# Attention feeding a feed-forward layer: scores in four chunks issued two at a time, tails padded to full tiles, one transpose for both tails, all engines in program order

## The chip, the cores and the metric

The kernel runs on one core of one Trainium2 chip. The metric is device time in microseconds (us), the median of several executions. The profile and the trace are those of one execution; their span is about 2 us shorter than the time of the same execution. Engines are named as in the profile: PE is the tensor engine's matmuls, PEld its weight loads, DVE the vector engine, ACT the scalar engine, POOL GpSimd, SP the Sync engine, whose queue (SPq) issues most transfers.

## The reference

Attention with a forget gate over 8 batches of 8 heads, 576 positions, 64 columns a head, followed by a feed-forward layer with SiLU over all 4,608 tokens:

```python
scores = q @ k.T / 8 + (cum[i] - cum[j])        # causal; cum = cumsum(log f)
attn   = softmax(scores)
x      = (attn @ v), heads side by side         # 4608 x 512
h      = x @ w_in                               # 512 x 2048
out    = (h * sigmoid(h)) @ w_out               # 2048 x 512, float32
```

Inputs are float32; the kernel computes in bf16. 576 is 4 tiles of 128 and a tail of 64.

## The kernel before

Work goes by pairs of heads, numbered 0 to 31, four to a batch. For each pair: load and cast q and k, transpose them on PE, copy the transposes to SBUF (`qkT`), multiply them (`scores`), take exp on ACT into `u`, mask on DVE. For each two pairs, `den` sums the weights, DVE takes reciprocals (`rec`), and eight transfers spread them over partitions (`rb<-rec`). `num` multiplies by v, and DVE multiplies by `rb` into `xT`. Between these steps the loop calls `fill`, which issues pieces of the feed-forward layer: 144 pieces of the first matmul (`hp`, then tanh on ACT and `gt` on DVE, the "gate work") and 144 of the second (`po`). A piece is four matmuls of 512 columns. `fill` can give nothing before the first batch is finished, which is at the end of pair 4.

Each partition gets four neighbouring rows of q or k (1 KB runs), so the transposes come out permuted, and the DVE copy puts the columns in order with a strided write:

```python
    def transposes(n):
        tp = psc.tile([P, 2, 1024], BF16, name="tp", tag="sc")
        for i in range(2):                       # q, k
            for j in range(NJ):
                nc.tensor.transpose(tp[:, i, j * P : (j + 1) * P], src[:, i, j, :], ident_bf[:, :])
            nc.tensor.transpose(                 # the tail, 64 rows
                tp[:, i, SM:S], tail[:, i, p * P : (p + 1) * P], ident_bf[:ST, :ST])
        t = qktp.tile([P, 2, S], BF16, name="qkT", tag="qkT")
        for i in range(2):
            nc.vector.tensor_copy(
                out=t[:, i, 0:SM].rearrange("r (p j) -> r j p", j=NJ),
                in_=tp[:, i, 0:SM].rearrange("r (j p) -> r j p", j=NJ))
        nc.vector.tensor_copy(out=t[:, :, SM:S], in_=tp[:, :, SM:S])
    # [cut] scores: three chunks of 512 columns, then the 64x64 tail "sd" with its own exp
    # [cut] den, num: tail matmuls with 64 rows
    for n in range(NU):                          # shortened
        scores(n, 0); fill(1)
        # [cut] casts of pair n+1 (POOL), loads of pair n+4 and of the next batch (SP)
        scores(n, 1); fill(1)
        scores(n, 2); fill(2)
        transposes(n + 1); fill(1)
        if n % 2 == 1:
            fill(1); den(n // 2); rec_part(n // 2, 0); fill(1); rec_part(n // 2, 1); fill(1)
        elif n >= 2:
            num(n - 2); fill(1); num(n - 1); fill(2); finished(n - 1)
```

Only PE runs in the order of the program; the Tile framework orders the other four queues.

The softmax here doesn't subtract the row's maximum and nothing guards it: scores larger than these inputs give would overflow.

## Time and profile before

448.99 us (3 runs, 445.46 to 449.27). The page of the profile, parts 1 and 2 (busy time with share of the span; then tenths busy in 40 equal slices of 11.2 us):

```profile
PE 390.3 (87%) x3013; PEld 177.7 (40%) x3013; DVE 290.5 (65%) x406; ACT 204.7 (46%) x312; POOL 97.5 (22%) x149
...
PE   2236676899979999999989998999899989999996
...
PEclk9999999999999999999999999999999999999999
DMA  8995959975666365425642423250203020400011
```

PE is 80% to full from slice 8 on, but for two slices, and 20 to 70% busy before; DMA is busiest just where PE is not.

From the trace I take the start of each pair, which is the start of its first scores matmul. Pairs 7 to 30 are regular: two pairs without gate work and two with it alternate. In the windows view, one such group of four pairs (columns: stretch, length, then busy time of each engine, PE clock, DMA share, GB/s):

```profile
175.58:188.77 13.19, 11.62 (x92) 5.40 (x92) 12.25 (x18) 7.62 (x12) 2.28 (x4) 1.00 0.33 85
188.77:199.05 10.28, 10.28 (x91) 4.50 (x91) 6.90 (x10) 4.27 (x6) 1.17 (x2) 1.00 0.37 106
199.05:210.78 11.73, 11.42 (x91) 5.23 (x92) 6.80 (x10) 4.27 (x6) 3.00 (x4) 1.00 0.48 140
210.78:221.07 10.29, 10.29 (x92) 4.50 (x92) 7.15 (x13) 7.23 (x12) 4.55 (x7) 1.00 0.83 193
```

Three of the four are filled by PE. The first, with gate work and two `num`, has DVE busy for 12.25 of 13.19 us.

The timeline of PE around a transposition (start, duration, line, operation, count). The durations shown overlap (190.38 + 1.04 lies beyond 191.35), so the distance from one start to the next is what counts:

```profile
190.38 1.04 PE L423 MATMUL po<-w_out_bf,gt 128*128 128x512 bf16 x4
191.35 0.39 PE L278 MATMUL sc<-qkT 64*128 64x320 bf16 x4
...
191.82 1.90 PE L423 MATMUL po<-w_out_bf,gt 128*128 128x512 bf16 x8
193.56 0.39 PE L235 MATMUL tp<-ident_bf,qkb 128*128 128x128 bf16 x4
193.88 0.20 PE L238 MATMUL tp<-ident_bf,qkt 64*128 64x64 bf16 x1
194.01 0.40 PE L235 MATMUL tp<-ident_bf,qkb 128*128 128x128 bf16 x4
194.34 0.20 PE L238 MATMUL tp<-ident_bf,qkt 64*128 64x64 bf16 x1
194.47 0.82 PE L423 MATMUL po<-w_out_bf,gt 128*128 128x512 bf16 x3
```

Eight full `po` matmuls before full transposes take 1.74 us, so four take 0.87; the four before 64-row scores take 0.97 (190.38 to 191.35). The change from `128*128` to `64*128` costs about 0.1 us. Below, this is called a mode switch, and also a drain; both names stand for this distance between starts, and what PE does in it the trace does not show. The transposes of the pair take 0.91 us (193.56 to 194.47).

The groups of DVE and ACT that matter (count, busy us, mean ns of one, idle before):

```profile
L285 ACT ACTIVATE u<-sc 128x1024 bf16<-128x1024 f32 x96 | 97.9, 1026 | 50.9 <-PE sc L278 39.8
L243 DVE COPY qkT<-tp 128x512 bf16<-128x512 bf16 x64 | 79.2, 1322 | 27.4 <-PE tp L238 27.4
L343 DVE RECIPROCAL rec<-dn 128x288 f32<-128x288 f32 x32 | 61.2, 1936 | 4.5 <-PE dn L331 4.5
```

And the first reciprocals, in the timelines of DVE and of the SP queue:

```profile
35.52 3.77 DVE L343 RECIPROCAL rec<-dn 128x288 f32<-128x288 f32 x2 [0.16 <-PE dn L331]
...
44.24 0.72 DVE L378 TENSOR_TENSOR xT<-nm,rb 128x576 bf16<-128x576 f32 x1
```

```profile
27.93 0.47 SPq L75 DMA_DIRECT2D kf<-in_k_dram  x1
39.31 5.02 SPq L351 DMA_DIRECT2D rb<-rec  x8
```

The reciprocals end at 39.3 us; the SP queue has issued nothing since 28.4 and issues `rb` at once.

### The profile page before, as it was taken

Reading aid. Unit: us, or ns where it says so; the run is one execution under the profiler, and the core shown is the slowest. Engines: PE = TensorE matmul, PEld = TensorE weight load, DVE = VectorE, ACT = ScalarE, POOL = GpSimd, SP = SyncE. Lnnn points to the kernel's source line nnn. Section 1 sums busy time; section 2 is a strip of 40 time slices with the busy share of each in tenths; the row PEclk is TensorE's granted clock in tenths of the full one; section 3 lists DMA queues with packets and bytes.
Section 4 is the critical chain, followed back from the end, with each engine's and each line's share of the span. In section 5 each row is a group of like instructions: output and inputs, shape, how many; then the busy total and the mean of one; then the engine's idle time right before and its main releaser. Section 6 shows DMA issues by size and latency. Waiting matters only on the chain.

```text
span 448.4 us, 7690 instructions
## 1 busy us (share of the span) xinstructions
PE 390.3 (87%) x3013; PEld 177.7 (40%) x3013; DVE 290.5 (65%) x406; ACT 204.7 (46%) x312; POOL 97.5 (22%) x149
## 2 busy tenths in 40 slices
PE   2236676899979999999989998999899989999996
PEld 1113332344434444444444444444444444444442
DVE  4668553966598649964996489647965794374310
ACT  3222323654464437443754375437543754264421
POOL 6573250361242151214221422111111000000000
PEclk9999999999999999999999999999999999999999
DMA  8995959975666365425642423250203020400011
GB/s 234 211 212 129 217 91 204 269 168 155 176 145 152 102 172 128 124 95 162 139 123 89 130 72 101 72 148 26 53 25 101 26 53 25 123 1 24 25 70 70
DMA packets 79156, 52.03 MB, mean 116 GB/s; under 512 B 49872, under 2 KB 70352, under 8 KB 79120
## 3 DMA queue, kind: packets, MB, share of 16 engines
q1 hardware_dynamic: 74896, 47.35, 40.4%
q0 software_dynamic: 4224, 4.19, 5.8%
q8 instruction: 23, 0.38, 0.4%
q14 instruction: 13, 0.11, 0.1%
HBM read 36.85 MB, written 9.44 MB: 103 GB/s over the span
## 4 chain that ended last, share of the span: by engine, by line
PE 54%; DVE 25%; ACT 11%; issue 5%; DMA 3%; SPq 1%; POOL 0%; DVEq 0%; ACTq 0%; POOLq 0%
PE po L423 28%; PE hp L396 11%; ACT u L285 7%; DVE qkT L243 7%; DVE gt L405 6%; DVE rec L343 6%; PE nm L366 5%; PE sc L278 3%; DVE u L298 3%; PE tp L235 3%; PE dn L331 2%; DMA rb<-rec 2%; ACT osb L432 2%; ACT th L404 2%; DVE u L302 1%
## 5 line engine op out<-in xcount | busy, mean ns | idle before, releaser
L396 PE MATMUL hp<-xT,w_in_bf 128*128 128x512 bf16 x576 | 141.7, 385 | 12.2 <-DVE gt L405 6.8
L423 PE MATMUL po<-w_out_bf,gt 128*128 128x512 bf16 x576 | 137.9, 380 | 0.0
L405 DVE SCALAR_TENSOR_TENSOR gt<-th,hp 128x512 bf16<-128x512 bf16 x144 | 94.9, 675 | 53.4 <-ACT th L404 53.0
L404 ACT ACTIVATE th<-hp 128x512 bf16<-128x512 f32 x144 | 86.1, 602 | 89.1 <-PE hp L396 81.6
L285 ACT ACTIVATE u<-sc 128x1024 bf16<-128x1024 f32 x96 | 97.9, 1026 | 50.9 <-PE sc L278 39.8
L243 DVE COPY qkT<-tp 128x512 bf16<-128x512 bf16 x64 | 79.2, 1322 | 27.4 <-PE tp L238 27.4
L396 PEld LDWEIGHTS <-w_in_bf 128*128 128x128 bf16 x576 | 50.9, 98 | 67.4 <-issue 16.5
L423 PEld LDWEIGHTS <-gt 128*128 128x128 bf16 x576 | 50.6, 98 | 58.9 <-issue 5.7
L432 ACT ACTIVATE osb<-po 128x512 f32<-128x512 f32 x36 | 21.5, 597 | 97.3 <-PE po L423 92.0
L343 DVE RECIPROCAL rec<-dn 128x288 f32<-128x288 f32 x32 | 61.2, 1936 | 4.5 <-PE dn L331 4.5
L95 POOL CAST qkb<-qf 128x512 bf16<-128x512 f32 x31 | 19.1, 615 | 197.3 <-issue 114.9
L278 PE MATMUL sc<-qkT 64*128 64x512 bf16 (+4 forms) x320 | 41.0, 323 | 23.6 <-ACT u L285 11.9
L298 DVE TENSOR_TENSOR u<-u,mask 128x768 bf16<-128x768 bf16 x32 | 22.2, 692 | 32.1 <-ACT u L285 32.1
L278 PEld LDWEIGHTS <-qkT 64*128 64x128 bf16 x320 | 13.5, 97 | 66.3 <-issue 51.2
L378 DVE TENSOR_TENSOR xT<-nm,rb 128x576 bf16<-128x576 f32 x32 | 23.8, 744 | 17.9 <-PE nm L366 11.5
L366 PE MATMUL nm<-u,vp 128*64 128x64 bf16 (+4 forms) x512 | 30.0, 264 | 4.4 <-DVE qkT L247 3.5
L366 PEld LDWEIGHTS <-vp 128*64 128x64 bf16 x512 | 19.5, 117 | 22.6 <-DVE qkT L247 10.6
L235 PE MATMUL tp<-ident_bf,qkb 128*128 128x128 bf16 x256 | 27.6, 236 | 0.7 <-ACT u L285 0.5
L235 PEld LDWEIGHTS <-qkb 128*128 128x128 bf16 x256 | 18.2, 104 | 8.6 <-issue 0.5
L95 POOL CAST qkb<-kf 128x512 bf16<-128x512 f32 x32 | 20.6, 643 | 3.0 <-DMA kf<-in_k_dram 3.0
L331 PE MATMUL dn<-u,w_bf 128*32 128x64 bf16 (+4 forms) x512 | 16.0, 261 | 5.9 <-DVE u L298 5.9
L331 PEld LDWEIGHTS <-w_bf 128*32 128x32 bf16 (+1 forms) x576 | 11.3, 99 | 17.1 <-issue 13.1
(79 smaller groups left out, 150.8 us busy)
## 6 DMA issues: line engine op xcount, KB each, us to landing
rb<-rec SPq DMA_DIRECT2D x128, 72.0 KB, 2.0
out_dram<-osb SPq DMA_DIRECT2D x36, 256.0 KB, 2.0
qf<-in_q_dram SPq DMA_DIRECT2D x32, 256.0 KB, 3.1
kf<-in_k_dram SPq DMA_DIRECT2D x32, 256.0 KB, 3.3
w_in_bf<-in_moe_w_in_dram POOLq DMA_DIRECT2D x4, 512.0 KB, 8.3
w_out_bf<-in_moe_w_out_dram POOLq DMA_DIRECT2D x4, 512.0 KB, 11.2
qtf<-in_q_dram SPq DMA_DIRECT2D x8, 128.0 KB, 3.9
ktf<-in_k_dram SPq DMA_DIRECT2D x8, 128.0 KB, 4.0
```

The source lines that it names most:

```text
L95: ins = engs[i].tensor_copy(out=t2[:, i, :, :].rearrange("p j (h d) -> p h j d", d=D), in_=t[:, :, :].rearrange("p h (j d) -> p h j d", d=D),)
L235: nc.tensor.transpose(tp[:, i, j * P : (j + 1) * P], src[:, i, j, :], ident_bf[:, :])
L243: nc.vector.tensor_copy(out=t[:, i, 0:SM].rearrange("r (p j) -> r j p", j=NJ), in_=tp[:, i, 0:SM].rearrange("r (j p) -> r j p", j=NJ),)
L278: nc.tensor.matmul(sc[:, i, col : col + q1 - q0], lhsT=t[r, 1, kb * P : (kb + 1) * P], rhs=t[r, 0, q0:q1], start=True, stop=True,)
L285: nc.scalar.activation(out=u[:, :, c * 512 : (c + 1) * 512], in_=sc[:, :, :], func=ACT.Exp, scale=scale)
L331: nc.tensor.matmul(dn[32 * j : 32 * j + 32, q0:q1], lhsT=w_bf[r, kb, bh : bh + 1].to_broadcast([nk, 32]), rhs=rhs, start=(kb == 0), stop=( ...
L343: nc.vector.reciprocal(out=rec[:, r], in_=dn[:, r])
L366: nc.tensor.matmul(nm[i * D : (i + 1) * D, q0:q1], lhsT=v_t[r, p, :] if kb == NM else vp[:, kb, 2 * p + i, :], rhs=(ut[r, :] if kb == NM e ...
L396: nc.tensor.matmul(hp[:, :], lhsT=w_in_bf[:, cc, fc * P : (fc + 1) * P], rhs=xT[:, cc, t0 : t0 + TG], start=(cc == 0), stop=(cc == NCC - 1),)
L404: nc.scalar.activation(out=th[:, :], in_=hp[:, :], func=ACT.Tanh, scale=0.5)
L405: nc.vector.scalar_tensor_tensor(out=gt[:, fc, :], in0=th[:, :], scalar=1.0, in1=hp[:, :], op0=ALU.add, op1=ALU.mult,)
L423: nc.tensor.matmul(po[:, :], lhsT=gt[:, fc, tb * P : (tb + 1) * P], rhs=w_out_bf[:, fc, :], start=(fc == 0), stop=(fc == NFC - 1),)
```

## The change

It aims at fewer 64-row visits on PE and a cheap qkT copy. q and k are loaded in natural order (256-byte runs), so one contiguous copy of 1,152 columns suffices. The q tail and k tail share a full 128-row transpose. The 64-row tail of `den` and `num` becomes a full tile whose upper half is masked to zero. Scores are 1,600 columns in four chunks of 400, issued two and two, with no separate tail. ACT copies the denominators out of PSUM before DVE takes reciprocals. All five engines run in program order.

```diff
-    ctx.enter_context(tc.manual_schedule(engines={mybir.EngineType.PE}))
+    ctx.enter_context(tc.manual_schedule(engines=set(ORDERED)))     # PE, ACT, DVE, POOL, SP
 # load_qk
-            t = stage.tile([P, 2, NJ * D], FP32, ...)
-            nc.sync.dma_start(out=t[:, :, :],
-                in_=src[b, 2 * p : 2 * p + 2, 0:SM, :].rearrange("h (p j) d -> p h (j d)", j=NJ))
+            t = stage.tile([P, NM, 2, D], FP32, ...)
+            for i in range(2):
+                nc.sync.dma_start(out=t[:, :, i, :],
+                    in_=src[b, 2 * p + i, 0:SM, :].rearrange("(c p) d -> p c d", p=P))
 # transposes
-            nc.tensor.transpose(tp[:, i, SM:S], tail[:, i, ...], ident_bf[:ST, :ST])
-        [three copies, two of them strided]
+        nc.tensor.transpose(tp[:, SM : SM + P], tbf[b][:, p * P : (p + 1) * P], ident_bf[:, :])
+        nc.vector.tensor_copy(out=t[:, :], in_=tp[:, 0:QKW])
 # den
+        nc.scalar.activation(out=rec[:, :], in_=dn[:, 0:S], func=ACT.Copy)
 # loop
         scores(n, 0)
+        scores(n, 1)
         fill(1)
 [cut: casts and loads of later pairs; w_in still at pair 2, w_out at pair 5 instead of 6]
-        scores(n, 1)
         fill(1)
         scores(n, 2)
-        fill(2)
+        scores(n, 3)
+        fill(2 if n % 2 == 0 else 1)
 [cut: also den and num tails, masks, v tails; num(n-2) and num(n-1) now side by side]
```

More of the change, by code (lines that the diff above doesn't have):

```diff
@@ L13 @@
 P = 128
+ET = mybir.EngineType
+ORDERED = (ET.PE, ET.Activation, ET.DVE, ET.Pool, ET.SP)
 @with_exitstack
@@ L59 @@
     pbig = ctx.enter_context(tc.tile_pool(name="pbig", bufs=4, space=bass.MemoryType.PSUM))
-    NJ = SM // P
     qst: dict[int, tuple] = {}
-    tst: dict[int, tuple] = {}
+    tst: dict[int, bass.AP] = {}
     vst: dict[int, list] = {}
@@ L67 @@
     tbf: dict[int, bass.AP] = {}
-    vbf: dict[int, tuple] = {}
+    vbf: dict[int, bass.AP] = {}
     def load_qk(n):
@@ L73, in load_qk @@
         for name, src in (("qf", q), ("kf", k)):
-            t = stage.tile([P, 2, NJ * D], FP32, name=name, tag=name, bufs=4)
-            nc.sync.dma_start(
-                out=t[:, :, :],
-                in_=src[b, 2 * p : 2 * p + 2, 0:SM, :].rearrange("h (p j) d -> p h (j d)", j=NJ),
-            )
+            t = stage.tile([P, NM, 2, D], FP32, name=name, tag=name, bufs=4)
+            for i in range(2):
+                nc.sync.dma_start(
+                    out=t[:, :, i, :],
+                    in_=src[b, 2 * p + i, 0:SM, :].rearrange("(c p) d -> p c d", p=P),
+                )
             ts.append(t)
@@ L82, in load_tails @@
     def load_tails(b):
-        ts = []
-        for name, src in (("qtf", q), ("ktf", k)):
-            t = stage.tile([ST, H, D], FP32, name=name, tag=name)
+        t = stage.tile([P, H, D], FP32, name="qktf", tag="qktf")
+        for i, src in enumerate((q, k)):
             nc.sync.dma_start(
-                out=t[:, :, :], in_=src[b, :, SM:S, :].rearrange("h s d -> s h d")
-            )
-            ts.append(t)
-        tst[b] = tuple(ts)
+                out=t[i * ST : (i + 1) * ST, :, :],
+                in_=src[b, :, SM:S, :].rearrange("h s d -> s h d"),
+            )
@@ L92, in cast_qk @@
+        tst[b] = t
     def cast_qk(n, engs):
-        t2 = conv.tile([P, 2, NJ, 2 * D], BF16, name="qkb", tag="qkb")
+        t2 = conv.tile([P, 2, NM, 2 * D], BF16, name="qkb", tag="qkb")
         for i, t in enumerate(qst.pop(n)):
-            ins = engs[i].tensor_copy(
-                out=t2[:, i, :, :].rearrange("p j (h d) -> p h j d", d=D),
-                in_=t[:, :, :].rearrange("p h (j d) -> p h j d", d=D),
+            engs[i].tensor_copy(
+                out=t2[:, i, :, :], in_=t[:, :, :, :].rearrange("p c h d -> p c (h d)")
@@ L98, in cast_qk, with load_v @@
             )
         qbf[n] = t2
-        return ins
     def cast_tails(b):
-        t2 = conv.tile([ST, 2, H * D], BF16, name="qkt", tag="qkt")
-        for i, t in enumerate(tst.pop(b)):
-            nc.gpsimd.tensor_copy(
-                out=t2[:, i, :], in_=t[:, :, :].rearrange("s h d -> s (h d)")
-            )
+        t2 = conv.tile([P, H * D], BF16, name="qkt", tag="qkt")
+        nc.gpsimd.tensor_copy(out=t2[:, :], in_=tst.pop(b)[:, :, :].rearrange("s h d -> s (h d)"))
         tbf[b] = t2
-    def load_v(b, c, h0, h1):
+    def load_v(b, c):
@@ L111, in load_v @@
         if b not in vst:
             vst[b] = [
-                stage.tile([P, H if i < NM else NP, D], FP32, name=f"vf{i}", tag=f"vf{i}")
-                for i in range(NM + 1)
-            ]
-        if c < NM:
-            nc.sync.dma_start(
-                out=vst[b][c][:, h0:h1, :],
-                in_=v[b, h0:h1, c * P : (c + 1) * P, :].rearrange("h p d -> p h d"),
-            )
-            return
-        for i in range(2):
-            nc.sync.dma_start(
-                out=vst[b][c][i * ST : (i + 1) * ST, h0 // 2 : h1 // 2, :],
-                in_=v[b, h0 + i : h1 : 2, SM:S, :].rearrange("h p d -> p h d"),
-            )
+                stage.tile([P, H, D], FP32, name=f"vf{i}", tag=f"vf{i}") for i in range(NM + 1)
+            ]
@@ L128 @@
+        r = slice(0, P) if c < NM else slice(ST, P)
+        nc.sync.dma_start(
+            out=vst[b][c][r, :, :],
+            in_=v[b, :, c * P : min(S, (c + 1) * P), :].rearrange("h p d -> p h d"),
+        )
     f_sb = setup.tile([BH, S], FP32, name="f_sb")
@@ L134 @@
     for c in range(NM + 1):
-        load_v(0, c, 0, H)
+        load_v(0, c)
     ident_bf = const.tile([P, P], BF16, name="ident_bf")
@@ L144 @@
     mask_t = const.tile([P, ST], BF16, name="mask_t")
-    for i in range(2):
-        make_upper_triangular(nc, mask_t[i * ST : (i + 1) * ST, :], val=1.0, diag=True)
+    nc.gpsimd.memset(mask_t[0:ST, :], 0.0)
+    make_upper_triangular(nc, mask_t[ST:P, :], val=1.0, diag=True)
     xT = const.tile([P, NCC, NT], BF16, name="xT")
@@ L199, with convert_v, k_off @@
     us: dict[int, tuple] = {}
-    def convert_v(b, c, h0, h1, eng):
+    def convert_v(b, c):
         if b not in vbf:
-            vbf[b] = (
-                vpool.tile([P, NM, H, D], BF16, name="vp", tag="vp"),
-                vpool.tile([P, NP, D], BF16, name="v_t", tag="v_t"),
-            )
-        vp, v_t = vbf[b]
-        vf = vst[b][c]
-        if c < NM:
-            eng.tensor_tensor(
-                out=vp[:, c, h0:h1, :],
-                in0=vf[:, h0:h1, :],
-                in1=w_bf[:, c, b * H + h0 : b * H + h1, None].to_broadcast([P, h1 - h0, D]),
-                op=ALU.mult,
-            )
-            return
-        for i in range(2):
-            r = slice(i * ST, (i + 1) * ST)
-            eng.tensor_tensor(
-                out=v_t[r, h0 // 2 : h1 // 2, :],
-                in0=vf[r, h0 // 2 : h1 // 2, :],
-                in1=w_bf[r, NM, b * H + h0 + i : b * H + h1 : 2, None].to_broadcast(
-                    [ST, (h1 - h0) // 2, D]
-                ),
-                op=ALU.mult,
-            )
+            vbf[b] = vpool.tile([P, NM + 1, H, D], BF16, name="vp", tag="vp")
+        vp = vbf[b]
+        r = slice(0, P)
+        if c == NM:
+            r = slice(ST, P)
+            nc.gpsimd.memset(vp[0:ST, NM, :, :], 0.0)
+        n = r.stop - r.start
+        nc.gpsimd.tensor_tensor(
+            out=vp[r, c, :, :],
+            in0=vst[b][c][r, :, :],
+            in1=w_bf[r, c, b * H : (b + 1) * H, None].to_broadcast([n, H, D]),
+            op=ALU.mult,
+        )
+    QKW = 2 * S
+    def k_off(kb):
+        return SM if kb == NM else S + ST + kb * P
     def transposes(n):
@@ L230, in transposes @@
         src = qbf.pop(n)
-        tail = tbf[b]
-        tp = psc.tile([P, 2, 1024], BF16, name="tp", tag="sc")
+        tp = psc.tile([P, 2048], BF16, name="tp", tag="sc")
         for i in range(2):
-            for j in range(NJ):
-                nc.tensor.transpose(
-                    tp[:, i, j * P : (j + 1) * P], src[:, i, j, :], ident_bf[:, :]
-                )
-            nc.tensor.transpose(
-                tp[:, i, SM:S], tail[:, i, p * P : (p + 1) * P], ident_bf[:ST, :ST]
-            )
@@ L241, in transposes @@
-        t = qktp.tile([P, 2, S], BF16, name="qkT", tag="qkT")
-        for i in range(2):
-            nc.vector.tensor_copy(
-                out=t[:, i, 0:SM].rearrange("r (p j) -> r j p", j=NJ),
-                in_=tp[:, i, 0:SM].rearrange("r (j p) -> r j p", j=NJ),
-            )
-        nc.vector.tensor_copy(out=t[:, :, SM:S], in_=tp[:, :, SM:S])
-        qkT[n] = t
-    UW = 3 * 512
-    def u_off(kb, qq):
-        if kb == 0:
-            return qq if qq < SM else 960 + qq - SM
-        if kb == 1:
-            return 512 + qq - 128
-        if kb == 2:
-            return 1024 + qq - 256
-        return 1344 + qq - 384
@@ L261 @@
-    CHUNKS = (
-        ((0, 0, 512, 0),),
-        ((1, 128, 576, 0), (0, 512, 576, 448)),
-        ((2, 256, 576, 0), (3, 384, 576, 320)),
-    )
+            for c in range(NM):
+                o = i * (S + ST) + c * P
+                nc.tensor.transpose(tp[:, o : o + P], src[:, i, c, :], ident_bf[:, :])
+        nc.tensor.transpose(
+            tp[:, SM : SM + P], tbf[b][:, p * P : (p + 1) * P], ident_bf[:, :]
+        )
+        t = qktp.tile([P, QKW], BF16, name="qkT", tag="qkT")
+        nc.vector.tensor_copy(out=t[:, :], in_=tp[:, 0:QKW])
@@ L267, in scores @@
+        qkT[n] = t
+    UO = [0]
+    for kb in range(NM + 1):
+        UO.append(UO[-1] + S - kb * P)
+    UW = UO[-1]
+    CW = UW // 4
     def scores(n, c):
         if c == 0:
-            u = upool.tile([P, 2, UW], BF16, name="u", tag="u")
-            ut = upool.tile([P, ST], BF16, name="ut", tag="ut")
-            us[n] = (u, ut)
-        u, ut = us[n]
+            us[n] = upool.tile([P, 2, UW], BF16, name="u", tag="u")
+        u = us[n]
         t = qkT[n]
         sc = psc.tile([P, 2, 512], FP32, name="sc", tag="sc")
-        for kb, q0, q1, col in CHUNKS[c]:
+        for kb in range(NM + 1):
+            lo, hi = max(UO[kb], c * CW), min(UO[kb + 1], (c + 1) * CW)
+            if lo >= hi:
+                continue
+            q0 = kb * P + lo - UO[kb]
@@ L278, in scores @@
                 nc.tensor.matmul(
-                    sc[:, i, col : col + q1 - q0],
-                    lhsT=t[r, 1, kb * P : (kb + 1) * P],
-                    rhs=t[r, 0, q0:q1],
+                    sc[:, i, lo - c * CW : hi - c * CW],
+                    lhsT=t[r, k_off(kb) : k_off(kb) + P],
+                    rhs=t[r, q0 : q0 + hi - lo],
                     start=True,
@@ L285, in scores @@
         nc.scalar.activation(
-            out=u[:, :, c * 512 : (c + 1) * 512], in_=sc[:, :, :], func=ACT.Exp, scale=scale
+            out=u[:, :, c * CW : (c + 1) * CW], in_=sc[:, :, 0:CW], func=ACT.Exp, scale=scale
         )
-        if c < 2:
+        if c % 2 == 0:
             return
-        sd = pbig.tile([P, ST], FP32, name="sd", tag="big")
-        for i in range(2):
-            r = slice(i * D, (i + 1) * D)
-            nc.tensor.matmul(
-                sd[r, :], lhsT=t[r, 1, SM:S], rhs=t[r, 0, SM:S], start=True, stop=True
-            )
-        nc.scalar.activation(out=ut[:, :], in_=sd[:, :], func=ACT.Exp, scale=scale)
-        d0 = u[:, :, :].rearrange("p i (c x) -> p (i c) x", x=512)[:, :, 0:P]
-        nc.vector.tensor_tensor(
-            out=d0, in0=d0, in1=mask[:, None, :].to_broadcast([P, 6, P]), op=ALU.mult
-        )
-        d1 = u[:, :, 1344 : 1344 + P]
-        nc.vector.tensor_tensor(
-            out=d1, in0=d1, in1=mask[:, None, :].to_broadcast([P, 2, P]), op=ALU.mult
-        )
-        nc.vector.tensor_tensor(out=ut[:, :], in0=ut[:, :], in1=mask_t[:, :], op=ALU.mult)
+        d = [u[:, :, UO[c - 1] : UO[c - 1] + P], u[:, :, UO[c] : UO[c] + P]]
+        for x in d:
+            nc.vector.tensor_tensor(
+                out=x, in0=x, in1=mask[:, None, :].to_broadcast([P, 2, P]), op=ALU.mult
+            )
+        if c == 3:
+            x = u[:, :, UO[NM] : UW]
+            nc.vector.tensor_tensor(
+                out=x, in0=x, in1=mask_t[:, None, :].to_broadcast([P, 2, ST]), op=ALU.mult
+            )
     def q_parts(kb):
@@ L310, in q_parts, with u_part @@
         yield SM, S
+    def u_part(n, i, kb, q0, q1):
+        o = UO[kb] - kb * P
+        return us[n][:, i, o + q0 : o + q1]
     recs: dict[int, bass.AP] = {}
@@ L322, in den @@
                     bh = b * H + 2 * p + i
-                    u, ut = us[n]
-                    r = slice(i * ST, (i + 1) * ST) if kb == NM else slice(0, P)
-                    nk = ST if kb == NM else P
-                    rhs = (
-                        ut[r, :]
-                        if kb == NM
-                        else u[:, i, u_off(kb, q0) : u_off(kb, q0) + q1 - q0]
-                    )
                     nc.tensor.matmul(
                         dn[32 * j : 32 * j + 32, q0:q1],
-                        lhsT=w_bf[r, kb, bh : bh + 1].to_broadcast([nk, 32]),
-                        rhs=rhs,
+                        lhsT=w_bf[:, kb, bh : bh + 1].to_broadcast([P, 32]),
+                        rhs=u_part(n, i, kb, q0, q1),
                         start=(kb == 0),
@@ L337, in den @@
                     )
-        dens[qd] = (dn, recp.tile([P, S], FP32, name="rec", tag="rec"))
+        rec = recp.tile([P, S], FP32, name="rec", tag="rec")
+        nc.scalar.activation(out=rec[:, :], in_=dn[:, 0:S], func=ACT.Copy)
+        dens[qd] = rec
     def rec_part(qd, part):
-        dn, rec = dens[qd]
+        rec = dens[qd]
         r = slice(part * S // 2, (part + 1) * S // 2)
-        nc.vector.reciprocal(out=rec[:, r], in_=dn[:, r])
+        nc.vector.reciprocal(out=rec[:, r], in_=rec[:, r])
         if part == 0:
@@ L358, in num @@
         b, p = divmod(n, NP)
-        u, ut = us.pop(n)
-        vp, v_t = vbf[b]
+        vp = vbf[b]
         nm = psc.tile([P, 1024], FP32, name="nm", tag="sc")
@@ L364, in num @@
                 for i in range(2):
-                    r = slice(i * ST, (i + 1) * ST)
                     nc.tensor.matmul(
                         nm[i * D : (i + 1) * D, q0:q1],
-                        lhsT=v_t[r, p, :] if kb == NM else vp[:, kb, 2 * p + i, :],
-                        rhs=(
-                            ut[r, :]
-                            if kb == NM
-                            else u[:, i, u_off(kb, q0) : u_off(kb, q0) + q1 - q0]
-                        ),
+                        lhsT=vp[:, kb, 2 * p + i, :],
+                        rhs=u_part(n, i, kb, q0, q1),
                         start=(kb == 0),
@@ L376, in num @@
                     )
+        us.pop(n)
         rb = recs.pop(n)
@@ L463 @@
         scores(n, 0)
+        scores(n, 1)
         fill(1)
         if n + 1 < NU:
-            last_cast = cast_qk(n + 1, (nc.gpsimd, nc.gpsimd))
+            cast_qk(n + 1, (nc.gpsimd, nc.gpsimd))
         if n + 4 < NU:
@@ L469 @@
         if n == 2:
-            with tc.issue_after(last_cast.ins):
-                for c in range(NM + 1):
-                    convert_v(0, c, 0, H, nc.gpsimd)
-                for i in range(WQ):
-                    load_w_in(i)
-        if n == 6:
-            with tc.issue_after(last_cast.ins):
-                for i in range(WQ):
-                    load_w_out(i)
+            for c in range(NM + 1):
+                convert_v(0, c)
+            for i in range(WQ):
+                load_w_in(i)
+        if n == 5:
+            for i in range(WQ):
+                load_w_out(i)
         if b + 1 < B:
@@ L482 @@
                 for c in range(NM + 1):
-                    load_v(b + 1, c, 0, H)
+                    load_v(b + 1, c)
             if p == 2:
@@ L486 @@
                 for c in range(2):
-                    convert_v(b + 1, c, 0, H, nc.gpsimd)
+                    convert_v(b + 1, c)
             if p == 3:
                 for c in range(2, NM + 1):
-                    convert_v(b + 1, c, 0, H, nc.gpsimd)
-        scores(n, 1)
+                    convert_v(b + 1, c)
         fill(1)
         scores(n, 2)
-        fill(2)
+        scores(n, 3)
+        fill(2 if n % 2 == 0 else 1)
         if n + 1 < NU:
             transposes(n + 1)
-        fill(1)
+        fill(2)
         if n % 2 == 1:
-            fill(1)
             den(n // 2)
             rec_part(n // 2, 0)
-            fill(1)
+            fill(2)
             rec_part(n // 2, 1)
@@ L506 @@
             num(n - 2)
-            fill(1)
             num(n - 1)
```

## The prediction

> **What bounds it now.** The page gives TensorE (PE) 390.3 us of 448.4 (87%), DVE 290.5, ACT 204.7. The stage table shows PE busy about 48 us of every 50 from 150 on but 5.6 to 14.1 in the first four stretches of 20. Three parts:
> - a start of about 65 us: no feed-forward work yet, each head pair a latency chain (scores, exp, transposes, qkT copies);
> - 27 head pairs bound by PE. In the timeline four pairs repeat every 45.5 us (10.66, 11.35, 10.66, 12.81; the last has gate work and reciprocals, so DVE, at about 11 us, limits it);
> - a feed-forward tail of about 78 us, untouched.
>
> **PE: the change removes mode switches.** [...] four 512-column matmuls take 862 ns before another of their kind, but 969 ns before 64-row scores, so about 107 ns a switch. Per pair, from start times:
> - Transposes: 912 ns now. Full ones start 56 ns apart, but the 64-row tails add about 100 ns going in and out, twice. Nine full ones: about 505. Saves 0.41 us.
> - Scores: seven switches now, four after. Columns stay 1,600. Saves 0.3 us.
> - num tail with 128 rows: one switch less, 0.11; the two num side by side: 0.21 per two pairs; den tail: 0.1 per two pairs.
> Together about 1.0 us a pair, on the critical path while PE binds.
>
> **DVE.** qkT costs 2 x 1.22 + 0.25 us now (512 elements written with stride). One contiguous copy of 1,152 bf16 from PSUM: 0.75 us [...], 1.3 [...] (estimates from the 252 ns for 128 elements and 744 for 576). Masks rise from three operations to five, about +0.25. Net about -1.3 us a pair, which should remove most of each fourth pair's stall of 1.5 to 2 us.
>
> **ACT.** Three exps of 1,024 (1.03 us) plus one of 64 (0.23) become four of 800: 0.84 each by the slope between 602 ns for 512 and 1,026 for 1,024. Even. The denominator's copy adds about 0.65 us per two pairs. ACT reaches about 8.7 us of a 10 us pair with tanh work: tight.
>
> **DMA.** q and k change from 1 KB packets (median 46 ns) to 256 B (18 ns, so 72 per KB): some 49,000 packets and 15 to 25 us of 16-engine time more over the span, most harmful in the first 60 us, where DMA is mostly 80 to 100% busy.
>
> **Sum.** Start: the chain of four exps, transposes and one short copy is about 7.5 us a pair against about 10.5; with DMA and GpSimd contention pair 5 starts near 55 instead of 65. Pairs 5 and 6: 27 instead of 31. 24 pairs at 10.45 instead of 11.43: 251 instead of 274. Tail 77. Total **410 us**, range 397 to 425. Faster by over 2% 0.94, within 0.045, slower 0.015.
>
> **Right or wrong shows in:** a pair's transposes taking about 0.5 us; steady pair periods of 9.6 to 10.8 us; DVE qkT near 0.75 or 1.3 us; first feed-forward matmul at 50 to 58 us; more DMA packets, near 128,000.
>
> **What would make it wrong:** strict program order making ACT or DVE wait at the head of its queue (masks behind the fourth exp, reciprocals before gates); transposes waiting for the third exp after only one filler in odd pairs; 256 B packets or the ordered SP queue delaying the start.

55, 27, 251 and 77 add to 410 us. The 107 ns of a switch rest on the two distances beside them. The 0.75 and 1.3 us for the copy are estimates from two durations of the before trace, 252 ns for a copy of 128 bf16 elements and 744 ns for a multiplication of 576 float32 columns: a fixed 190 ns and 0.96 ns an element fit both if the bf16 copy takes half of that per element, and 1,152 elements then come to 0.74 us, or to 1.30 at the whole. That the copy would go at the half was the assumption; no run had shown it.

## The result, and the profile after

420.95 us (4 runs, 420.44 to 422.15) against 447.23 for the kernel before (4 runs); ratio 0.9416, 95% interval 0.9356 to 0.9476: faster. A ratio here is the mean time of one kernel's fast runs over that of the other's fast runs of the same rounds, so it is not quite the ratio of the medians quoted.

The page after, the same lines:

```profile
PE 359.0 (86%) x3109; PEld 176.8 (42%) x3109; DVE 249.9 (60%) x406; ACT 213.2 (51%) x328; POOL 95.9 (23%) x140
...
PE   1650456989998999899989998999899989999996
...
PEclk9995565999999999999999999999999999999999
DMA  8999699761696179617861696169614021300111
```

The first slices of PE are as empty as before, and now PE's granted clock drops to 0.5 to 0.6 in slices 4 to 7. It does not decide the time: of four runs three show a mean clock near 0.95 and one 1.00, with times of 420.4 to 422.2 and 421.4 us. Why the clock drops here and not in the kernel before, no run tests.

One group of four pairs in the windows view:

```profile
162.02:173.16 11.14, 10.39 (x94) 5.26 (x94) 11.09 (x20) 7.26 (x12) 3.92 (x6) 1.00 0.58 138
173.16:183.91 10.75, 9.61 (x96) 4.54 (x95) 5.52 (x10) 4.98 (x7) 1.31 (x2) 1.00 0.39 95
183.91:194.06 10.15, 10.15 (x96) 5.12 (x95) 5.31 (x10) 4.22 (x6) 1.18 (x2) 1.00 0.40 104
194.06:203.85 9.79, 9.59 (x96) 4.53 (x95) 7.17 (x13) 8.03 (x13) 4.72 (x6) 1.00 1.08 234
```

41.8 us against 45.5. The first fell by 2.05 us, the third by 1.58; the second rose by 0.47, with PE idle for over a microsecond in it. PE around that pair:

```profile
173.16 0.34 PE L247 MATMUL sc<-qkT 64*128 64x400 bf16 x2
174.64 0.35 PE L247 MATMUL sc<-qkT 64*128 64x176 bf16 x4 [1.14 <-ACT u L254]
174.92 1.90 PE L379 MATMUL po<-w_out_bf,gt 128*128 128x512 bf16 x8
...
178.08 0.61 PE L219 MATMUL tp<-ident_bf,qkb 128*128 128x128 bf16 x8
178.53 0.22 PE L220 MATMUL tp<-ident_bf,qkt 128*128 128x128 bf16 x1
178.59 1.89 PE L379 MATMUL po<-w_out_bf,gt 128*128 128x512 bf16 x8
```

The transposes take 0.51 us (178.08 to 178.59) instead of 0.91. The bracket in the second line says that PE was idle for 1.14 us until an exp ended. The groups:

```profile
L254 ACT ACTIVATE u<-sc 128x800 bf16<-128x800 f32 x128 | 101.2, 847 | 53.9 <-PE sc L247 43.9
...
L224 DVE COPY qkT<-tp 128x1152 bf16<-128x1152 bf16 x32 | 24.0, 750 | 4.2 <-PE tp L220 4.1
```

The copies fell from 87 us in all to 24: one copy of 1,152 contiguous elements took 750 ns, where one of 512 strided ones had taken 1,322. Of the prediction's two estimates it is the lower, 0.75 us. ACT's exps took 847 ns (predicted 840).

The start, in the timelines of DVE and the SP queue:

```profile
22.18 3.77 DVE L304 RECIPROCAL rec<-rec 128x288 f32<-128x288 f32 x2 [0.57 <-ACT rec L298]
...
44.72 0.76 DVE L334 TENSOR_TENSOR xT<-nm,rb 128x576 bf16<-128x576 f32 x1 [14.87 <-DMA rb<-rec]
```

```profile
26.20 5.90 SPq L112 DMA_DIRECT2D vf_226<-in_v_dram  x1
32.16 4.12 SPq L77 DMA_DIRECT2D qf<-in_q_dram  x2
...
40.33 5.02 SPq L312 DMA_DIRECT2D rb<-rec  x8
```

The reciprocals end at 26.0 us, 13 us earlier than before. But the queue is stuck: loads for batch 1 that nobody needs yet take up to 5.9 us each to issue, loads of q and k follow, and `rb` goes out at 40.3. The first `xT` is written at 44.7 us; before it was 44.2. Pairs 0 and 1 went from 12.3 and 10.8 us to 4.9 and 5.7, and pair 2 from 10.6 to 23.9. All that the faster pairs won was given back as one wait.

Where the time went (starts of pairs and the span from the trace, us; each rounded by itself):

| | before | after | predicted |
|---|---|---|---|
| start of pair 5 | 64.9 | 65.3 | 55 |
| pairs 5 and 6 | 30.8 | 24.1 | 27 |
| pairs 7 to 30 | 274.9 | 251.2 | 251 |
| pair 31 to the end | 77.6 | 78.2 | 77 |
| span / sum | 448.4 | 418.7 | 410 |

### The profile page after: what moved, and what is told of

The parts are those of the page before. It is cut to its first block, busy times and chain, and to the rows that moved or that the text cites. A ratio compares the mean times of both kernels' runs of the same rounds, so it can differ in the third digit from the quotient of the medians.

```text
span 418.7 us, 8037 instructions
## 1 busy us (share of the span) xinstructions
PE 359.0 (86%) x3109; PEld 176.8 (42%) x3109; DVE 249.9 (60%) x406; ACT 213.2 (51%) x328; POOL 95.9 (23%) x140
## 3 DMA queue, kind: packets, MB, share of 16 engines
q1 hardware_dynamic: 124944, 47.36, 50.1%
## 4 chain that ended last, share of the span: by engine, by line
PE 50%; DVE 17%; SPq 11%; ACT 9%; DMA 6%; issue 5%; POOL 1%; ACTq 0%; DVEq 0%; POOLq 0%
PE po L379 26%; PE hp L352 14%; DVE gt L361 7%; DVE rec L304 6%; ACT u L254 6%; SPq L77 4%; SPq L312 4%; PE nm L325 3%; PE sc L247 3%; PE dn L290 2%; PE tp L219 2%; ACT th L360 2%; DMA out_dram<-osb 2%; SPq L112 1%; DVE u L261 1%
## 5 line engine op out<-in xcount | busy, mean ns | idle before, releaser
L352 PE MATMUL hp<-xT,w_in_bf 128*128 128x512 bf16 x576 | 137.6, 383 | 0.1
L254 ACT ACTIVATE u<-sc 128x800 bf16<-128x800 f32 x128 | 101.2, 847 | 53.9 <-PE sc L247 43.9
L261 DVE TENSOR_TENSOR u<-u,mask 128x256 bf16<-128x256 bf16 x128 | 42.4, 346 | 57.7 <-ACT u L254 57.4
L247 PE MATMUL sc<-qkT 64*128 64x176 bf16 (+5 forms) x512 | 40.0, 269 | 36.2 <-DVE xT L334 20.0
L304 DVE RECIPROCAL rec<-rec 128x288 f32<-128x288 f32 x32 | 61.1, 1934 | 15.7 <-ACT rec L298 15.7
L247 PEld LDWEIGHTS <-qkT 64*128 64x128 bf16 x512 | 20.3, 99 | 67.4 <-issue 63.0
L325 PEld LDWEIGHTS <-vp 128*64 128x64 bf16 x576 | 21.0, 114 | 20.4 <-issue 15.9
L224 DVE COPY qkT<-tp 128x1152 bf16<-128x1152 bf16 x32 | 24.0, 750 | 4.2 <-PE tp L220 4.1
L219 PE MATMUL tp<-ident_bf,qkb 128*128 128x128 bf16 x256 | 21.9, 235 | 3.8 <-ACT u L254 2.9
L103 POOL CAST qkt<-qktf 128x512 bf16<-128x512 f32 x8 | 4.9, 616 | 58.4 <-DMA qktf<-in_k_dram 58.4
L298 ACT ACTIVATE rec<-dn 128x576 f32<-128x576 f32 x16 | 10.4, 651 | 13.1 <-PE dn L290 12.9
```

The costliest lines, as they stand in the source:

```text
L219: nc.tensor.transpose(tp[:, o : o + P], src[:, i, c, :], ident_bf[:, :])
L224: nc.vector.tensor_copy(out=t[:, :], in_=tp[:, 0:QKW])
L247: nc.tensor.matmul(sc[:, i, lo - c * CW : hi - c * CW], lhsT=t[r, k_off(kb) : k_off(kb) + P], rhs=t[r, q0 : q0 + hi - lo], start=True, sto ...
L254: nc.scalar.activation(out=u[:, :, c * CW : (c + 1) * CW], in_=sc[:, :, 0:CW], func=ACT.Exp, scale=scale)
L261: nc.vector.tensor_tensor(out=x, in0=x, in1=mask[:, None, :].to_broadcast([P, 2, P]), op=ALU.mult)
L304: nc.vector.reciprocal(out=rec[:, r], in_=rec[:, r])
```

## The experiments

Twelve kernels ran, all on the same inputs and all accepted by the comparison with the reference. A "group" below is four times the mean of pairs 7 to 30. All times are medians of fast runs; one run of strided_copy, the profiled one, was slow and is left out. The before kernel ran at medians of 449.2 to 449.6 us beside them, so ratios to it compare better than times do.

| kernel | us | ratio to before | pair 3 starts | pair 5 starts | group |
|---|---|---|---|---|---|
| before | 447.23 | 1 | 46.0 | 64.9 | 45.8 |
| after | 420.95 | 0.942 | 45.5 | 65.3 | 41.9 |
| rb_first | 453.19 | 1.005 | 34.8 | 63.4 | 47.7 |
| pack1k_wrong | 418.66 | 0.929 | 42.5 | 62.8 | 41.9 |
| w_in_late | 415.78 | 0.925 | 35.0 | 59.8 | 41.8 |
| before_ordered | 449.69 | 0.999 | 38.8 | 57.4 | 47.3 |
| two_visits | 427.57 | 0.952 | 45.9 | 66.2 | 42.8 |
| one_score | 418.86 | 0.933 | 46.3 | 66.1 | 41.6 |
| strided_copy | 437.67 | 0.976 | (slow profile) | | |
| spread | 406.07 | 0.903 | 34.7 | 55.8 | 41.2 |
| before_short_copy | 433.95 | 0.968 | 41.2 | 58.1 | 44.3 |
| spread_rot | 399.79 | 0.891 | 34.2 | 56.5 | 40.2 |
| spread_odd1 | 399.93 | 0.892 | 34.9 | 55.7 | 40.4 |
| pe_order_only | 432.99 | 0.963 | 58.5 | 75.1 | 42.7 |

### The start: order, packets, or the weight load?

**rb_first** moves loads behind the reciprocals in program order:

```diff
-        if n + 4 < NU: load_qk(n + 4)            # after the casts, early in the pair
-            if p == 0: load_tails(b + 1); [five] load_v(b + 1, c)
+        # at the end of the pair
+        if n + 4 < NU: load_qk(n + 4)
+        if b + 1 < B and p == 1: load_tails(b + 1); [five] load_v(b + 1, c)
```

> After kernel, only the order of the Sync queue changed: the loads of the next batch's tails and v move from the start of each first pair to the end of each second pair, and each pair's q and k loads to the end of the pair, so the broadcast of the first reciprocals (rb) is issued before them. Theory A (the 14.7 us stall of pair 2 is rb standing behind prefetches in the queue): rb is issued within 1 us of the reciprocals, near 26 us instead of 40.3; pair 3 starts at 30 to 36 us instead of 45.5, pair 5 at 52 to 60 instead of 65.3, and the total falls by 5 to 13 us to 408 to 416. Rival B (the DMA engines simply cannot deliver the bytes of the start sooner, whatever the order): pair 5 still starts at 63 to 67 us because a later load is waited for instead, and the total stays within 4 us of 421.

453.19 us, a miss in total, yet theory A held for the stall itself: `rb` was issued at 26.01 us and pair 3 began at 34.8 instead of 45.5. Pair 5 began at 63.4, which is in rival B's range, so this run alone does not exclude B. What went wrong is the edit's own doing. POOL's queue is in order too, and its cast of the next tails comes at a fixed place:

```profile
42.35 0.61 POOL L103 CAST qkt<-qktf 128x512 bf16<-128x512 f32 x1 [16.47 <-DMA qktf<-in_k_dram]
```

POOL now waited 16.5 us for tails that were requested later, with the casts of q and k for the next pair behind it. The same happened once in every batch (one pair in four took 17 us), so the gain was lost several times over. Moving a load means moving what waits for it.

**pack1k_wrong** loads q and k in 1 KB runs as before and leaves the columns permuted. The result is wrong. It passed the comparison all the same; with inputs scaled by 0.1 the scores are tiny, which would explain it, but that was not tested.

```diff
-            t = stage.tile([P, NM, 2, D], ...);  in_=...rearrange("(c p) d -> p c d", p=P)
+            t = stage.tile([P, 2, NM * D], ...); in_=...rearrange("(p j) d -> p (j d)", j=NM)
```

> Wrong result on purpose: the after kernel with q and k loaded four rows to a partition (1 KB packets as in the kernel before) and not put back in order. Everything else has the same shape. Theory C (256 B packets [...] make the start slow): the Sync issues at 26 to 40 us, which took 2.5 to 6 us each, drop below 1.5 us; rb is issued near 30 us; pair 5 starts 6 us or more earlier and the total is 410 to 415. Theory A or B (order, or bytes with the w_in burst): packets matter little, pair 5 moves by less than 4 us, total 417 to 421. Packets in total should fall from 129 thousand to about 80 thousand.

Pair 3 came 3.0 us earlier and pair 5 2.6; 418.66 us, ratio 0.929. So theory C is a small part: `rb` began to issue at 29.7, but its eight issues took 12.1 us, where they took 5.0 in the kernels before and after. The ratio improved by 1.2 points.

**w_in_late** issues the four loads of w_in at pair 4:

```diff
-        if n == 2: ...; [four] load_w_in(i)
+        if n == 4: [four] load_w_in(i)
```

> After kernel with the four w_in loads issued at pair 4 instead of pair 2. Theory D (the 4 MB w_in burst at 22 to 26 us on the GpSimd queue is what fills the DMA engines and so delays rb): pair 2's stall falls from 14.7 us to under 5 and pair 3 starts before 38 us; but the first feed-forward matmul then may wait for w_in, so the total may gain little or lose. If pair 2 still stalls over 10 us, the burst is not the cause.

Pair 3 at 35.0, so theory D holds: without the 4 MB burst the same loads in the same order left the queue free at 29.6 us, when `rb` was issued. The burst then struck pair 4 (18.0 us). Net 415.78 us, ratio 0.925.

Order and burst are thus two handles on one cause: in the first 40 us the DMA engines are loaded to the full (DMA share 1.08 and 1.26 in the first two stretches of 20 us of the after kernel; the view adds the times of packets, so it can exceed 1), and `rb` was late when anything not yet needed was ahead of it: it was issued at 40.3 us in the after kernel, at 29.7 in pack1k_wrong and 29.6 in w_in_late, but at 26.0 in rb_first, where those loads came behind it.

**spread** uses both handles and moves the waiters along:

```diff
             if p == 0: load_tails(b + 1)         # v no longer here
             if p == 2: cast_tails(b + 1)
-                       [two] convert_v(b + 1, c)
-            if p == 3: [three] convert_v(b + 1, c)
+            if p == 3: [five] convert_v(b + 1, c)
 # after rec_part(n // 2, 1)
+            if p == 1 and b + 1 < B: [five] load_v(b + 1, c)
-        if n == 2: [four] load_w_in;  if n == 5: [four] load_w_out
+        w_in parts: one at pair 2, one at 3, two at 4;  w_out parts: two at pair 5, two at 6
```

> After kernel with the start's transfers put in the order of need: v of the next batch is loaded after the first rb of the batch, its casts and multiplications on GpSimd moved one or two pairs later so that its queue does not wait for them, w_in issued in four parts over pairs 2 to 4, w_out over pairs 5 and 6. Theory A plus D (the start is bound by what stands ahead of rb on the DMA engines: unneeded prefetches and the w_in burst): pair 3 starts at 28 to 33 us, pair 5 at 48 to 56, steady groups stay at 41.8, total 405 to 413. Rival B (bytes): pair 5 still starts after 60 us, because w_in or q and k are waited for, total above 416.

406.07 us, ratio 0.903. `rb` goes out when the reciprocals end, and v behind it:

```profile
26.06 5.26 SPq L312 DMA_DIRECT2D rb<-rec  x8
31.42 7.46 SPq L112 DMA_DIRECT2D vf<-in_v_dram  x5
```

Pair 3 began at 34.7, later than the expected 28 to 33, pair 5 at 55.8, at the upper end of what was expected, and rival B is out. Groups fell by 0.7 us as well, which was not expected: the pair with gate work and two `num` went from 11.14 to 10.31 us in most groups. The after trace shows why, in the timelines of DVE, POOL and PE in such a pair, and of DVE in pair 30:

```profile
167.14 0.90 DVE L261 TENSOR_TENSOR u<-u,mask 128x256 bf16<-128x256 bf16 x2
167.97 0.63 DVE L266 TENSOR_TENSOR u<-u,mask_t 128x128 bf16<-128x128 bf16 x1
...
167.28 0.62 POOL L96 CAST qkb<-qf 128x512 bf16<-128x512 f32 x1 [2.50 <-PE tp L220]
167.84 0.67 POOL L96 CAST qkb<-kf 128x512 bf16<-128x512 f32 x1
...
170.51 0.89 PE L325 MATMUL nm<-u,vp 128*64 128x512 bf16 x18 [0.75 <-DVE qkT L224]
...
335.38 0.49 DVE L261 TENSOR_TENSOR u<-u,mask 128x256 bf16<-128x256 bf16 x2
```

POOL's casts of q and k run just while DVE masks. The five masks of the pair then add to 2.17 us instead of 1.35, DVE, which is without a pause here, comes to the qkT copy that much later, and PE waits 0.75 us for its buffer. Pair 30 of the same run is of the same kind, but POOL has no work left: its masks add to 1.35 us and the pair takes 10.32, with the same matmuls. In spread POOL does nothing at all in most of these pairs.

### The steady state: mode switches, copy, order

**two_visits** puts the two 64-row transposes back, into columns that nobody reads:

```diff
             for c in range(NM): ...
+            nc.tensor.transpose(tp[:, QKW + i * ST : QKW + (i + 1) * ST],
+                                tbf[b][0:ST, p * P : (p + 1) * P], ident_bf[:ST, :ST])
```

> After kernel with two extra 64-row transposes of 64 columns in each pair, one behind the four q transposes and one behind the four k transposes, into columns that nobody reads; the result stays right. They put back exactly the two 64-row visits that the padded tail removed. Theory of the prediction (each visit costs two drains of about 100 ns besides its 27 ns of columns): transposes of a pair take about 0.96 us instead of 0.50, steady groups of four pairs grow by 1.5 to 1.9 us from 41.8 (part may be absorbed where the tensor engine already waits), total 429 to 434. Rival (the gain in the steady state comes from DVE and waits, not from drains): a group grows by less than 0.6 us, total 421 to 425.

```profile
180.61 0.39 PE L219 MATMUL tp<-ident_bf,qkb 128*128 128x128 bf16 x4
180.93 0.20 PE L220 MATMUL tp<-ident_bf,qkt 64*128 64x64 bf16 x1
181.06 0.40 PE L219 MATMUL tp<-ident_bf,qkb 128*128 128x128 bf16 x4
181.39 0.20 PE L220 MATMUL tp<-ident_bf,qkt 64*128 64x64 bf16 x1
181.53 0.23 PE L225 MATMUL tp<-ident_bf,qkt 128*128 128x128 bf16 x1
181.59 1.89 PE L384 MATMUL po<-w_out_bf,gt 128*128 128x512 bf16 x8
```

0.98 us instead of 0.51, so a visit costs PE 0.23 us, as read before. The total, 427.57, lies below the expected range and clearly above the rival's. A group grew by 0.9 us, not by the 1.9 of PE time, but not because waits took up half of it. Three of the four pairs grew by 0.48 us each (10.74 to 11.22, 10.15 to 10.63, 9.79 to 10.27), all that PE spends more. The fourth, with gate work and two `num`, fell from 11.14 to 10.68: with the later transposes POOL's casts came when the masks were nearly done, which add to 1.34 us, and the collision described under spread was gone. Against the 10.32 without a collision it grew too, by 0.36. So in these runs the switches cost in time nearly all of what they cost PE, and the smaller sum is an accident of timing.

**one_score** issues the chunks one at a time:

```diff
-        scores(n, 0); scores(n, 1); fill(1)
+        scores(n, 0); fill(1); scores(n, 1)
         ...
-        scores(n, 2); scores(n, 3); fill(2 if n % 2 == 0 else 1)
+        scores(n, 2); fill(1); scores(n, 3)
+        if n % 2 == 0: fill(1)
```

> After kernel with the four score chunks issued one at a time, a feed-forward piece between them, as the kernel before did with its three, instead of two and two. Four mode switches a pair more. Theory of the prediction: about 0.43 us a pair, groups of four 43.2 to 43.8, total 430 to 434. Rival: the pairing of chunks itself makes waits for exps (1.1 to 1.3 us stalls are seen behind the first chunk of some pairs), so unpairing costs less than 0.2 us a pair, total 418 to 426.

418.86 us, the rival. Groups 41.6 instead of 41.9 with four switches a pair more. The pair that had waited 1.14 us for an exp lost that wait (10.74 to 10.12 us), the third of the group paid for its switches (10.15 to 10.57). Issuing scores two at a time, as the change does, earned nothing.

**strided_copy** and **before_short_copy** are the two cross cases: the change without the short copy, and the short copy without the rest of the change.

```diff
 # strided_copy: after, with 1 KB loads as in pack1k_wrong, and
-        nc.vector.tensor_copy(out=t[:, :], in_=tp[:, 0:QKW])
+        for o in (0, S + ST): [strided copy of 512 columns]
+        nc.vector.tensor_copy(out=t[:, SM : SM + P], in_=tp[:, SM : SM + P])
 # before_short_copy: before, result wrong on purpose
-        [two strided copies and one of the tails]
+        nc.vector.tensor_copy(out=t[:, :, :], in_=tp[:, :, 0:S])
```

> After kernel with the old layout of q and k (1 KB packets) and the two strided qkT copies of before on DVE; right result. Theory (the short copy takes DVE off the limit in pairs with gate work and reciprocals, and nothing else): DVE qkT costs 2.7 us a pair instead of 0.75, pairs without gate work keep their 10.1 to 10.8 us, pairs with it grow, groups of four 43 to 46 us, total 425 to 440. If the copy did not matter, groups stay at 41.8 and the total at 416 to 421 as with 1 KB packets and no reordering.

> Wrong result on purpose: the kernel before with its three qkT copies (two strided) replaced by one contiguous copy of both halves, so that the columns stay permuted. The other half of the pair with strided_copy (the change without the short copy). Theory (in steady state the strided copies cost only where DVE is the limit, the pairs with gate work): the pair of 13.2 us falls to about 11.7, the other three keep 10.3, 11.7 and 10.3, groups 44.0; pairs 0 to 4 become shorter but wait for rb instead; total 436 to 443. If the two parts of the change add, before minus this is about 8 to 13 us and the rest of the 28 us is drains. If the copy alone gives most of the gain, the total is under 430.

Ratios: neither 1; short copy alone 0.968; all but the short copy 0.976; both, with the same 1 KB packets (pack1k_wrong), 0.929. The two parts alone give 3.2 and 2.4 points, together 7.1, so they help each other. In the steady state before_short_copy came out as expected: its four pairs take 10.3, 11.7, 10.3 and 11.8 us, so only the pair at DVE's limit fell. Its total, 433.95, lies below the expected 436 to 443, because pair 5 also began 6.9 us earlier. The profile of strided_copy fell into the slow state, so I don't compare its pairs; where the two parts help each other is not shown there. The next run shows one place.

**before_ordered** puts all engines of the kernel before in program order:

```diff
-    tc.manual_schedule(engines={mybir.EngineType.PE})
+    tc.manual_schedule(engines={ET.PE, ET.Activation, ET.DVE, ET.Pool, ET.SP})
-            with tc.issue_after(last_cast.ins):      # twice; not allowed in program order
```

> Kernel before with nothing but all five engines in program order (the two issue_after blocks, which that forbids, dropped). It tells how much of the gain is scheduling alone. Theory of the prediction (the gain is mode switches and the shorter qkT copy): 440 to 455 us, within 2% of before, steady groups of four pairs near 45.5 us. Rival (program order is itself the gain): 420 to 435 us.

449.69 us, ratio 0.999, but as the sum of two opposite moves: pair 5 started 7.5 us earlier, and groups were 1.5 us longer. All of the 1.5 lies in the pair at DVE's limit, which takes up to 15.9 us instead of 13.2, while the other three keep 10.3, 11.7 and 10.3. So with the strided copies program order costs time in steady state, and with the short one (pe_order_only, below) it does not.

**pe_order_only** is the reverse, the after kernel with only PE ordered:

```diff
-    tc.manual_schedule(engines=set(ORDERED))
+    tc.manual_schedule(engines={ET.PE})
```

> The after kernel with only the tensor engine in program order, as the kernel before had it; the other four queues are ordered by Tile again. Theory (the order of the four queues decides nothing in steady state, since before_ordered came out at the time of before): groups of four 41 to 43 us, total within 2% of 421, the difference lying in the start, where Tile issues w_in about 12 us earlier. Rival (program order is needed once the drains are gone, because masks and gates compete on DVE): groups over 43.5, total over 430.

432.99 us: the rival's number, but neither reason. The start lost 10 us (pair 5 at 75.1), the rest lies in a few long pairs. The expectation saw w_in come earlier, but not what it would cost, nor that w_out would too: POOL issued the first at 8 to 13 us and the second at 27 to 36, 8 MB in all, pair 2 took 37 us, and `rb` was issued at 53.6. Program order is worth about 2 points here, most of it in the start, where these loads are the visible difference.

### A wait for a buffer, and the best version

The second chunk of scores waited for the first chunk's exp. **spread_rot**, built on spread, gives the two big PSUM buffers names and takes them in turn:

```diff
-    psc = tc.tile_pool(name="psc", bufs=2, ...)      # tiles with tag="sc"
+    psc = tc.tile_pool(name="psc", bufs=1, ...)      # tiles with tag=psc_tag(): "sc1", "sc0", "sc1", ...
```

> The kernel with the start's transfers in order of need, and the two big PSUM buffers taken strictly in turn (a name for each) instead of as Tile's pool hands them out. Theory E (the 1.14 us wait of the second score chunk for the first exp, in each odd pair without gate work, comes from the pool giving both chunks the same buffer): that wait goes, the 10.74 us pair becomes 9.4 to 9.8, groups fall from 41.0 to 39.7 to 40.1, total 397 to 401. Rival (the wait is the other buffer's, being read by DVE): groups stay near 41.0 and the total at 405 to 407.

```profile
161.18 0.35 PE L253 MATMUL sc<-qkT 64*128 64x176 bf16 x4 [0.19 <-DVE xT L340]
```

Theory E held. The wait is now 0.19 us, and for DVE's reading of the other buffer. Groups 40.2 us, a little above the expected 39.7 to 40.1, 399.79 us in all, ratio 0.891 (0.884 to 0.897).

**spread_odd1**, also built on spread, leaves the pool and covers the wait with a filler in odd pairs:

```diff
         scores(n, 0)
+        if n % 2 == 1: fill(1)
         scores(n, 1)
-        fill(1)
+        if n % 2 == 0: fill(1)
```

> The same kernel with the pool as it was, but in odd pairs a feed-forward piece between the first and the second score chunk. It covers the same wait with work, for two switches more: the 10.74 us pair becomes 9.7 to 10.0, the odd pair with gate work 9.8 to 10.0, groups 40.1 to 40.4, total 400 to 403, so a little above strict turns if theory E holds, and below it if E fails.

399.93 us, ratio 0.892: the same within the interval. Either of the two is the best version, 5% faster than the after kernel.

## Why the prediction was right, and where it was off

The range, 397 to 425, held the result, and so did "faster". Point by point:

- **PE's savings: right.** The trace shows a pair's transposes at 0.51 us (predicted 0.505), two `num` side by side at 1.52 us where each took 0.94, and `den` at 0.81 instead of 0.92. PE's busy time in the group shown fell from 43.61 to 39.74 us, 0.97 a pair (predicted about 1.0). two_visits shows that such a visit is paid for in time, nearly in full: two of them took 0.47 us of PE, and three of four pairs grew by 0.48.
- **Scores: right on PE, wrong in effect.** The prediction counted 0.3 us a pair for issuing chunks two at a time. PE was spared that, but the second chunk then waited for a buffer, and one_score shows the pairing worth nothing. spread_rot turns part of it into time.
- **The short copy: right.** 750 ns, the lower of the two estimates, and before_short_copy gives the forecast relief in the DVE-bound pair. What the prediction did not see is that the copy and the rest of the change help each other.
- **Steady pairs: 251 us predicted, 251.2 measured.** This is partly luck: its own terms, 1.0 us a pair on PE and most of a stall of 1.5 to 2 us in each fourth pair, add to about 1.4 a pair, and the sum took 0.98 without saying why. In the group shown PE's idle time stayed near 2 us (1.88 before, 2.09 after): the old stall went, and two waits came that nobody had forecast, 1.14 us for the buffer and 0.75 where POOL's casts and DVE's masks meet.
- **The start: the term that failed.** "Pair 5 starts near 55 instead of 65" measured 65.3. The chain did shorten, to 4.9 and 5.7 us a pair where 7.5 was estimated. But the sum carried a chain through pairs 0 to 4, and what the start waits for is a transfer: the first `xT` came at 44.2 us before and 44.7 after, there with DVE idle for 14.87 us until `rb` had landed. The prediction named 256-byte packets and the SP queue as risks without putting a number on them. The runs put one: spread recovers 9.5 us at pair 5 by the order and the spacing of transfers, with 256-byte packets as they are; 1 KB packets alone recover 2.6.
- **DMA: under-sized.** The queue's share in the page went from 40.4% of 448.4 to 50.1% of 418.7 us, which is 29 us more (predicted 15 to 25).
- A smaller slip: the sum was one of spans, set against a time, which is 2 us longer.

What stays open: where strided_copy, the change without the short copy, loses its time, as its profile was slow; and what the full tails of `den` and `num`, ACT's copy of the denominators and the earlier w_out are worth in time, as no run takes one of them back alone.

## What to carry to other kernels

When the chain at the start of a kernel gets shorter, look for what its results have to queue behind: here a reciprocal finished 13 us earlier, and its 72 KB transfers then stood behind prefetches and a weight load that nobody needed yet. Where queues run in program order, as all five do in the after kernel, order transfers by when they are needed, and move their consumers in the other queues with them (in rb_first one cast left in its place held POOL's queue for 16.5 us). Count mode switches on PE by the distances between starts; here they were about 0.1 us each and were paid nearly in full. Read an experiment pair by pair before explaining its sum: one collision that went away hid half of what two_visits cost. And check that two chunks issued together really get two buffers.

## Measured on the way

- A mode switch on PE was about 0.1 us each way: 0.23 us for a 64-row visit with 27 ns of columns (an estimate: 64/512 of the 1.74/8 us of a full matmul).
- A copy on DVE from PSUM that wrote bf16 to SBUF with a stride of 4 elements took 1,322 ns for 512 elements, 2.6 ns each, where 1,152 contiguous ones took 750, 0.65 each. DVE's multiplication into `xT`, which also reads PSUM, took 744 ns for 576 columns, 1.3 ns each; so the stride alone may not be the whole difference, and no run separates the causes.
- In the before trace the median 256-byte packet of the SP queue took 18 ns and the 1 KB packet 46, so 256-byte runs took 57% more time per byte.
- An issue held its queue for very different times. In the after trace the load of the last 64 rows of v took 1.15 us to issue at 15.7 us for batch 0 (DMA share 1.08 from 0 to 20 us), and 5.90 us at 26.2 us for batch 1 (1.26 from 20 to 40 us), with all later transfers of the queue behind it.
